# Cosine attention and a highway layer on one core: gate and highway products in PSUM, weights cast by DMA, last tiles in the score banks, late x turned by DMA, loads held back

## The chip, the cores and the metric

The kernel runs on one NeuronCore of a Trainium2 chip. The metric is the device time of one execution in microseconds. The profile's span, from the first to the last instruction, is about 2 us shorter than the device time.

## The reference

```python
# attention: q, k, v are (8, 12, 448, 64), float32; tau = 0.1
q_n = q / (norm(q) + 1e-6);  k_n = k / (norm(k) + 1e-6)
attn = softmax(q_n @ k_n.T / tau)              # over 448 keys
x = (attn @ v) as 3584 tokens x 768            # heads side by side
# highway layer: w_h, w_t are (768, 768), b_t is (768)
H = maximum(x @ w_h, 0)
T = 1 / (1 + exp(-(x @ w_t + b_t)))
out = T * H + (1 - T) * x                      # (3584, 768), float32
```

## The kernel before

The program names a *quad* Q: four heads of one batch element, 24 in all. A quad's q and k arrive by DMA as 32-bit tiles `raw`; sums of squares and an inverse root (Newton steps on VectorE) give `rs`; the product `qn` of `raw` and `rs` is made on GpSimd; `qT` is its transpose, by TensorE for the first four quads and by DMA for the others. Then come seven steps of scores (`sp`, two PSUM buffers of two banks each) with an exponential on ScalarE (`e`), the product with v (`u`, one buffer of two banks), and the division into `x`.

[...] 4 for `sp`, 2 for `u`, and 2 for `pt`, which the transposes of x (`xp`) and the highway products share.

```python
s_ps = pool("s_ps", 2, space=PS)
u_ps = pool("u_ps", 1, space=PS)
p_ps = pool("p_ps", 2, space=PS)
```

The 28 highway tiles of 128 tokens are numbered in order, three for each batch element and one of the leftover rows (`xtail`) for each pair of them. For each tile x is turned by TensorE, copied to SBUF, and multiplied by four half weights. The ones column of v holds 2.0, so that x is kept as x/2: the gate then is (1 + tanh(z))/2 with z from the product itself, and b_t enters halved as a seventh matmul with a row of ones.

```python
def tr():
    loc["xp"] = p_ps.tile([128, CC, 128], FP16, name="xp", tag="pt")
    for c in range(CC):                                                     # CC = 6
        nc.tensor.transpose(loc["xp"][:, c, :], xf()[:, c * 128 : (c + 1) * 128], ident[:, :])   # L729
def ev():
    loc["xT"] = xt_p.tile([128, CC, 128], FP16, name="xT")
    nc.vector.tensor_copy(loc["xT"][:, :, :], loc["xp"][:, :, :])           # L733
...
for qi, (w_i, mh) in enumerate(((1, 0), (0, 0), (1, 1), (0, 1))):           # w_i 1: gate, 0: highway
    ...
    nc.tensor.matmul(loc["pt", qi][:, :],                                   # L760, 128 x 384
        lhsT=loc["xT"][:, cc, :] if cc < CC else ones_row[:, :],
        rhs=w_f[w_i][:, cc, ms] if cc < CC else bth[:, ms], ...)
    ...
    nc.scalar.activation(loc["tt"][:, ms], loc["pt", qi][:, :], AF.Tanh)    # L780, w_i 1
    nc.vector.scalar_tensor_tensor(                                         # L785, w_i 0
        out=loc["hm"][:, ms], in0=loc["pt", qi][:, :], scalar=0.0,
        in1=xf()[:, ms], op0=ALU.max, op1=ALU.subtract)
...
nc.vector.scalar_tensor_tensor(                                             # L801
    out=loc["th", mh][:, :], in0=loc["tt"][:, ms], scalar=1.0,
    in1=loc["hm"][:, ms], op0=ALU.add, op1=ALU.mult)
nc.vector.scalar_tensor_tensor(                                             # L809
    out=loc["o"][:, ms], in0=xf()[:, ms], scalar=2.0, in1=loc["th", mh][:, :],
    op0=ALU.mult, op1=ALU.add)
```

So out = 2(x/2) + (1 + t)(max(h, 0) - x/2). Weights come as twelve loads into three staging buffers, and VectorE casts each to 16 bits:

```python
nc.sync.dma_start(st["wst", i][:, :], src[cc * 128 : (cc + 1) * 128, :])           # L302
nc.vector.tensor_copy(w_f[1 - i // CC][:, i % CC, :], st["wst", i][:, :])          # L305
```

The squares of k are made by GpSimd for quads under FOLD (VectorE for quad 0), and VectorE reduces all 64 of each group. From FOLD on, ScalarE squares both q and k, GpSimd adds halves twice (lines 397 and 403), and VectorE reduces 16:

```python
eng = "ACT" if t == 0 or Q >= FOLD else "POOL" if Q else "DVE"
```

All operations are put down with a duration, a due time and their dependences, and a list scheduler in Python fixes each engine's order while the program is built; on the chip that order is kept.

```python
k = (max(s, t + self.NEAR[e]), o.pri, o.n)       # s: earliest start, pri: due time
```

Of the kernel before, what the change touches and what calls it, by code (L numbers as in the profile page):

```python
# [20 lines left out]
class Plan:  # L21
# [7 lines left out]
    NEAR = {"PE": 100, "ACT": 100, "DVE": 60, "POOL": 60, "SP": 60}  # L29
# [23 lines left out]
    def run(self):  # L53
# [20 lines left out]
        while back:  # L74
            o = back.pop()
            due = 1e9 if o.pri is None else o.pri[0] if isinstance(o.pri, tuple) else o.pri
            for c in outs[o.n] if not isinstance(o.pri, tuple) else ():
                lat = o.dur + self.LAT[o.eng] + (o.size + 2000 if o.eng == "SP" else 0)
                due = min(due, c.pri - (self.SLACK * lat / 1000 if o in c.deps else 0))
            o.pri = due  # L80
            for d in o.deps + o.after:
                users[d.n] -= 1
                if not users[d.n]:
                    back.append(d)

        def arm(o):
            r = 0
            for d in o.deps:
                r = max(r, d.done + (100 if d.eng == o.eng else self.LAT[d.eng]))
            for d in o.after:  # L90
                r = max(r, d.start)
            if o.eng == "SP":
                r += 300
            ready[o.eng].append((r, o))
# [9 lines left out]
        while len(order) < len(self.ops):  # L104
            best = None
            for e, L in ready.items():
                if not L:
                    continue
                t = t_eng[e]
                pick = None  # L110
                for r, o in L:
                    s = max(t, r)
                    if e == "DVE" and o.kind == "lock":
                        s = max(s, port[0])
                    elif e == "POOL":
                        s = max(s, port[1])
                    elif e == "SP" and len(lanes) >= 8:
                        s = max(s, lanes[-8])
                    if e == "SP":
                        s = max(s, dma_free - 5000)  # L120
                    k = (max(s, t + self.NEAR[e]), o.pri, o.n)
                    if pick is None or k < pick[0]:
                        pick = (k, s, r, o)
                if best is None or pick[1] < best[1]:
                    best = pick
            _, s, r, o = best
            e = o.eng
            ready[e].remove((r, o))
            end = s + o.dur
            if e == "PE":  # L130
                if o.kind != mode:
                    end += self.SWITCH
                mode = o.kind
            elif e == "POOL":
                port[0] = end
            elif e == "DVE" and o.kind == "lock":
                port[1] = end
            t_eng[e] = end
            o.start, o.done = s, end
            if e == "SP":  # L140
                dma_free = max(dma_free, end + 900) + o.size
                o.done = dma_free + 1100
                lanes.append(o.done)
            order.append(o)
            for c in outs[o.n]:
                left[c.n] -= 1
                if not left[c.n]:
                    arm(c)
# [7 lines left out]
def kernel(  # L156
# [30 lines left out]
    wst_p = pool("wst", N_W)  # L187
# [23 lines left out]
    bt_raw = const.tile([1, DM], FP32)  # L211
    ones_row = const.tile([128, 128], FP16)
    NV = 2
    FOLD = 6
    PAIR = 0
    NEWT = 8
    LEVELS = 2
    PIECES = 2
    vm_b = [const.tile([128, 6, C, 66], FP16, name=f"vm{i}") for i in range(NV)]
# [36 lines left out]
    def load_qk(Q):  # L256
# [4 lines left out]
        for t in range(2):  # L261
# [10 lines left out]
            o = op("SP", 60 if Q == 0 and t else 550, None, wait, f, size=1300)  # L272
# [5 lines left out]
    def load_v(b):  # L278
        ring, wait = P.buf("vr", N_VR)
        st["ring_vr", b] = ring  # L280

        def f():
            st["vr", b] = vraw_p.tile([128, 6, C * D], FP32, name="vr")
            nc.sync.dma_start(
                st["vr", b][:, :, :],
                v[b].rearrange("n (p c) d -> (n p) (c d)", c=C).rearrange("(i x) f -> x i f", x=128),
            )

        o = op("SP", 600, None, wait, f, size=4000)
        ring.append(o)  # L290
        st["gotv", b] = o
# [3 lines left out]
    def load_w(i):  # L295
        ring, wait = P.buf("w", N_W)

        def f():
            st["wst", i] = wst_p.tile([128, DM], FP32, name="wst")
            cc = i % CC  # L300
            src = (moe_w_t, moe_w_h)[i // CC]
            nc.sync.dma_start(st["wst", i][:, :], src[cc * 128 : (cc + 1) * 128, :])  # L302

        def g():
            nc.vector.tensor_copy(w_f[1 - i // CC][:, i % CC, :], st["wst", i][:, :])  # L305

        a = op("SP", 430, (12 + 1.8 * i,), wait, f, size=1300)
        c = op("DVE", 470, (16 + 1.8 * i,), [a], g, kind="lock")
        ring += [a, c]
        w_done[1 - i // CC].append(c)  # L310

    def load_b():
        def f():
            nc.sync.dma_start(bt_raw[:1, :], moe_b_t)

        def g():
            nc.vector.tensor_single_scalar(bth[:1, :], bt_raw[:1, :], 0.5, ALU.mult)

        a = op("SP", 430, (20,), [], f, size=50)
        w_done[1].append(op("DVE", 470, (25,), [a, o_fb], g))  # L320
# [217 lines left out]
    def cast_v(b):  # L538
# [3 lines left out]
        for i in range(NQ):  # L542
# [5 lines left out]
            outs.append(op("DVE", 540, None, wait + [o_fv[b % NV], st["gotv", b]], f,  # L548
# [162 lines left out]
    def ffn(b, t, F):  # L711
# [11 lines left out]
        ringp, waitp = P.buf("pt", 2)  # L723
# [11 lines left out]
        a = op("PE", 300, None, need + waitp, tr, kind="full")  # L735
        c = op("DVE", 470, None, [a] + waitt, ev)
        ringp += [a, c]
        ringt.append(c)
        ring_x.append(a)
        return lambda later: quarters(b, t, F, loc, c, ringt, ring_x, xf, later)  # L740

    def quarters(b, t, F, loc, c, ringt, ring_x, xf, later):
        ringf, waitf = P.buf("ff", N_FF)
        ringo, waito = P.buf("o", N_O)
        last = {}
        for qi, (w_i, mh) in enumerate(((1, 0), (0, 0), (1, 1), (0, 1))):
            ms = slice(mh * MH, (mh + 1) * MH)
            if qi == 2:
                later()
            ringq, waitq = P.buf("pt", 2)  # L750
            prev = None
            when = F + 1.6 * qi
            groups = ((0, 1, 2), (3, 4, 5)) if w_i == 0 else ((0, 1, 2), (3, 4, 5, 6))
            mms = []
            for gi, grp in enumerate(groups):
                def mm(grp=grp, w_i=w_i, ms=ms, qi=qi):
                    if grp[0] == 0:
                        loc["pt", qi] = p_ps.tile([128, MH], FP32, name="pt", tag="pt")
                    for cc in grp:
                        nc.tensor.matmul(  # L760
                            loc["pt", qi][:, :],
                            lhsT=loc["xT"][:, cc, :] if cc < CC else ones_row[:, :],
                            rhs=w_f[w_i][:, cc, ms] if cc < CC else bth[:, ms],
                            start=(cc == 0), stop=(cc == CC - 1 + w_i),
                        )
                m = op("PE", 163 * len(grp), when + 0.5 * gi,
                       [c] + ([("first", mms[:1])] if mms else waitq) + w_done[w_i], mm, kind="full")
# [4 lines left out]
            def first():  # L772
                if "tt" not in loc:
                    loc["tt"] = ff_p.tile([128, DM], FP16, name="tt")
                    loc["hm"] = ff_p.tile([128, DM], FP16, name="hm")

            if w_i == 1:
                def fa(qi=qi, ms=ms):
                    first()
                    nc.scalar.activation(loc["tt"][:, ms], loc["pt", qi][:, :], AF.Tanh)  # L780
                e = op("ACT", 390, None, [mms[-1]] + waitf, fa)
            else:
                def fa(qi=qi, ms=ms):
                    first()
                    nc.vector.scalar_tensor_tensor(  # L785
                        out=loc["hm"][:, ms], in0=loc["pt", qi][:, :], scalar=0.0,
                        in1=xf()[:, ms], op0=ALU.max, op1=ALU.subtract,
                    )
                e = op("DVE", 470, None, [mms[-1]] + waitf, fa)
            ringq.append(e)  # L790
            ringf.append(e)
            ring_x.append(e)
            last[w_i, mh] = e
        fin = []
        for mh in range(2):
            ms = slice(mh * MH, (mh + 1) * MH)
            ringh, waith = P.buf("th", N_FF)

            def ft(ms=ms, mh=mh):
                loc["th", mh] = ff_p.tile([128, MH], FP16, name="th")  # L800
                nc.vector.scalar_tensor_tensor(  # L801
                    out=loc["th", mh][:, :], in0=loc["tt"][:, ms], scalar=1.0,
                    in1=loc["hm"][:, ms], op0=ALU.add, op1=ALU.mult,
                )

            def fo(ms=ms, mh=mh):
                if mh == 0:
                    loc["o"] = out_p.tile([128, DM], FP32, name="o")
                nc.vector.scalar_tensor_tensor(  # L809
                    out=loc["o"][:, ms], in0=xf()[:, ms], scalar=2.0, in1=loc["th", mh][:, :],  # L810
                    op0=ALU.mult, op1=ALU.add,
                )

            e1 = op("DVE", 470, F + 3.5 + 3.2 * mh, [last[0, mh], last[1, mh]] + waith, ft, kind="lock")
            e2 = op("DVE", 470, F + 4 + 3.2 * mh, [e1] + ([("first", fin[:1])] if fin else waito), fo, kind="lock")
            ringh += [e1, e2]
            ringf += [e1]
            ringo.append(e2)
            ring_x.append(e2)
# [14 lines left out]
    for Q in range(NQUAD):  # L834
# [3 lines left out]
        if Q == 1:  # L838
            for i in range(2 * CC):
# [23 lines left out]
    for b in range(B):  # L863
        f0 = slot_t[NQ * (b + 1)] + 5
        for t in [0, 1, 2] + ([3] if b % 2 else []):
            todo.append((b, t, f0 + 6.3 * t))
# [46 lines left out]
```

## Time and profile before

| | |
|---|---|
| device time, median of 3 runs | 314.18 us (312.53 to 314.8) |
| span of the profiled execution | 312.4 us |
| mean granted TensorE clock | 0.95 |
| DMA traffic | 58.59 MB, mean 188 GB/s |
| first and last exponential, start | 17.5 and 279.4 us |
| first and last highway matmul, start | 58.4 and 306.0 us |
| last product qn on GpSimd, start | 242.3 us |

The page gives busy times of the engines: PE is TensorE's matmuls, PEld its weight loads, DVE is VectorE, ACT ScalarE, POOL GpSimd, SP SyncE, which issues most DMAs. A busy PE is not PE at its peak, as matmuls are pipelined and their ends are modelled. The chain is the work that ended last, followed back from the last instruction to what released each step. A name such as L785 is a line of the kernel, and "out<-in" are its tiles.

### The profile page before, as it was taken

What the parts mean: (1) busy time and instruction counts of PE and PEld (TensorE: products, weight loads), DVE (VectorE), ACT (ScalarE), POOL (GpSimd) and SP (SyncE); (2) the same over time, 40 slices, a digit from 0 to 9 for tenths busy, and PEclk for the clock granted to TensorE, in tenths of its full rate; (3) what the DMA queues carried; (4) which work ended last, traced back from release to release, by engine and by line L of the source; (5) the groups of instructions that cost most, each with busy time, mean ns of one, the idle gap of its engine ahead of it and who ended that gap; (6) DMA issues with size and microseconds to landing.
All of it is one profiled execution on the core that took longest, in us unless ns stands there. A gap on an engine that the chain in (4) does not pass through costs nothing.

```text
span 312.4 us, 10165 instructions
## 1 busy us (share of the span) xinstructions
PE 252.9 (81%) x4312; PEld 144.3 (46%) x4312; DVE 256.6 (82%) x527; ACT 203.0 (65%) x267; POOL 179.8 (58%) x180
## 2 busy tenths in 40 slices
PE   0175485798786999889995999979888999998992
PEld 0133253354442555445543555545554555565551
DVE  2999997779976799899979777999998666666773
ACT  4175669378681897798789577977776767661110
POOL 0375789957993389957986869599559100000000
PEclk9999777599997899999999799999999999999997
DMA  7999945998998719992993299766624352201213
GB/s 268 406 344 327 370 126 159 368 294 270 229 242 275 266 25 241 245 352 43 237 263 148 40 290 282 253 111 111 111 68 86 125 65 69 78 23 37 101 51 101
DMA packets 62319, 58.59 MB, mean 188 GB/s; under 512 B 38721, under 2 KB 57153, under 8 KB 62274
## 3 DMA queue, kind: packets, MB, share of 16 engines
q1 hardware_dynamic: 62002, 57.49, 65.5%
q8 instruction: 33, 0.54, 0.7%
q10 hardware_dynamic: 272, 0.46, 0.4%
q14 instruction: 12, 0.10, 0.1%
HBM read 37.75 MB, written 11.01 MB: 156 GB/s over the span
## 4 chain that ended last, share of the span: by engine, by line
DVE 42%; PE 41%; POOL 9%; issue 4%; DMA 2%; ACT 1%; DVEq 0%; POOLq 0%; ACTq 0%
PE pt L760 26%; PE u L629 7%; DVE n L370 6%; PE sp L578 6%; POOL qn L489 5%; DVE th L801 5%; DVE vm L544 5%; DVE x L680 4%; DVE o L809 4%; DVE hm L785 4%; DVE ta L449 2%; POOL fold L397 2%; PE xp L729 2%; DVE ta L451 1%; DMA raw<-in_q_dram 1%
## 5 line engine op out<-in xcount | busy, mean ns | idle before, releaser
L589 ACT ACTIVATE e<-sp 128x896 f16<-128x896 f32 x168 | 144.9, 920 | 56.8 <-PE sp L578 56.7
L760 PE MATMUL pt<-w,xT 128*128 128x384 f16 x672 | 135.0, 335 | 9.7 <-DVE hm L785 7.8
L489 POOL TENSOR_TENSOR qn<-raw,rs 128x448 f16<-128x448 f32 x92 | 101.3, 1133 | 27.3 <-DVE rs L453 18.0
L760 PEld LDWEIGHTS <-xT 128*128 128x128 f16 x672 | 61.1, 99 | 62.5 <-issue 29.5
L629 PE MATMUL u<-vm,e 64*128 64x65 f16 x2688 | 57.8, 196 | 15.3 <-DVE x L680 14.0
L629 PEld LDWEIGHTS <-e 64*128 64x128 f16 x2688 | 49.1, 97 | 37.5 <-DVE x L680 18.3
L578 PE MATMUL sp<-qT,qT 64*64 64x448 f16 x672 | 54.1, 391 | 9.3 <-DVE qT L519 5.9
L397 POOL TENSOR_TENSOR fold<-sq 128x448 f32<-128x448 f16 x36 | 40.4, 1136 | 21.7 <-ACT sq L346 21.7
L780 ACT ACTIVATE tt<-pt 128x384 f16<-128x384 f32 x56 | 27.7, 494 | 34.6 <-PE pt L760 34.2
L785 DVE SCALAR_TENSOR_TENSOR hm<-pt,x 128x384 f16<-128x384 f32 x48 | 26.6, 554 | 25.5 <-PE pt L760 25.3
L346 ACT ACTIVATE sq<-raw 128x896 f16<-128x896 f32 x42 | 40.3, 963 | 10.3 <-DMA raw<-in_q_dram 9.1
L801 DVE SCALAR_TENSOR_TENSOR th<-tt,hm 128x384 f16<-128x384 f16 x56 | 42.1, 752 | 3.1 <-DVE ta L451 0.3
L809 DVE SCALAR_TENSOR_TENSOR o<-x,th 128x384 f32<-128x384 f16 x48 | 38.4, 799 | 0.8
L578 PEld LDWEIGHTS <-qT 64*64 64x64 f16 x672 | 14.2, 108 | 32.5 <-issue 23.4
L403 POOL TENSOR_TENSOR fold<-fold 128x224 f32<-128x224 f32 x36 | 27.9, 793 | 0.7
L680 DVE TENSOR_TENSOR x<-u,rd 128x384 f16<-128x384 f32 x48 | 24.8, 550 | 0.6
L544 DVE CAST vm<-vr 128x896 f16<-128x896 f32 x24 | 24.2, 1026 | 0.0
L370 DVE TENSOR_REDUCE n<-sq 128x7 f32<-128x448 f16 x24 | 13.9, 606 | 6.3 <-ACT sq L346 4.3
L760 PE MATMUL pt<-bth,ones_row 128*128 128x384 f16 x56 | 18.7, 333 | 0.0
L513 PE MATMUL tp<-ident,qn 128*128 128x128 f16 x56 | 6.2, 283 | 15.0 <-DVE qn L489 14.1
L729 PE MATMUL xp<-ident,x 128*128 128x128 f16 x144 | 13.1, 224 | 4.2 <-DVE x L680 4.2
L662 DVE RECIPROCAL rd<-u 128x12 f32<-128x12 f32 (+1 forms) x48 | 9.6, 201 | 7.6 <-PE u L629 6.9
(34 smaller groups left out, 133.6 us busy)
## 6 DMA issues: line engine op xcount, KB each, us to landing
raw<-in_q_dram SPq DMA_DIRECT2D x24, 448.0 KB, 4.9
vr<-in_v_dram SPq DMA_DIRECT2D x8, 1344.0 KB, 8.7
raw<-in_k_dram SPq DMA_DIRECT2D x23, 448.0 KB, 6.3
out_dram<-o SPq DMA_DIRECT2D x24, 384.0 KB, 3.1
wst<-in_moe_w_t_dram SPq DMA_DIRECT2D x6, 384.0 KB, 6.6
wst<-in_moe_w_h_dram SPq DMA_DIRECT2D x6, 384.0 KB, 5.4
out_dram<-o SPq DMA_DIRECT2D x8, 192.0 KB, 2.7
qT<-qn SPq DMA_TRANSPOSE x40, 4.6
```

Source lines behind the costliest of these rows:

```text
L346: nc.scalar.activation(o, i, AF.Square)
L397: nc.gpsimd.tensor_add(st["fold", Q, t][:, g, :], sq[:, g, 0 : D // 2], sq[:, g, D // 2 : D])
L489: (nc.vector if eng == "DVE" else nc.gpsimd).tensor_mul(st["qn", Q, t][:, :, :].rearrange("p c (h d) -> p h c d", h=2)[:, h0:h1, c0:c1, :] ...
L544: nc.vector.tensor_copy(vm[:, 2 * i : 2 * i + 2, :, 0:D], st["vr", b][:, 2 * i : 2 * i + 2, :].rearrange("p i (c d) -> p i c d", c=C),)
L578: nc.tensor.matmul(sp[64 * half : 64 * half + 64, h, 0:S].rearrange("x (c p) -> x c p", c=C), lhsT=kT[hp, ci, 64 * half : 64 * half + 64], ...
L589: nc.scalar.activation(e[:, o : o + 2 * S].rearrange("x (a p c) -> x a p c", a=2, c=C), st["sp", Q, ci][:, :, 0:S].rearrange("x a (c p) -> ...
L629: nc.tensor.matmul(u[:, s, slot * (D + 1) : (slot + 1) * (D + 1)], lhsT=e[sp, o : o + 128], rhs=vm[sp, 2 * qd + h, c, 0 : D + 1], start=(c ...
L680: nc.vector.tensor_mul(st["x", b][:, :, 4 * qd : 4 * qd + 4, :].rearrange("p t (h s) d -> p t h s d", s=2)[:, :, :, s, :], u[:, s, :, 0:D] ...
L760: nc.tensor.matmul(loc["pt", qi][:, :], lhsT=loc["xT"][:, cc, :] if cc < CC else ones_row[:, :], rhs=w_f[w_i][:, cc, ms] if cc < CC else b ...
L785: nc.vector.scalar_tensor_tensor(out=loc["hm"][:, ms], in0=loc["pt", qi][:, :], scalar=0.0, in1=xf()[:, ms], op0=ALU.max, op1=ALU.subtract,)
L801: nc.vector.scalar_tensor_tensor(out=loc["th", mh][:, :], in0=loc["tt"][:, ms], scalar=1.0, in1=loc["hm"][:, ms], op0=ALU.add, op1=ALU.mult,)
L809: nc.vector.scalar_tensor_tensor(out=loc["o"][:, ms], in0=xf()[:, ms], scalar=2.0, in1=loc["th", mh][:, :], op0=ALU.mult, op1=ALU.add,)
```

## The change

It has several parts.

1. *Gate and highway products.* out = max((1+t)h, 0) - (t-1)(x/2). VectorE makes the carry term g = (t-1)(x/2) in SBUF, multiplies h by (1+t) in place in PSUM, and then takes the maximum and subtracts g. It is meant to keep only one operation of a half tile with both inputs in SBUF.
2. *Weights.* Four DMAs issued by GpSimd cast while they load; the staging buffers and the casts on VectorE are gone.
3. *Last tiles.* Tiles 21 to 27 put gate and highway products side by side in one score buffer of two banks. Their bias is added by VectorE, from a copy of b_t on all partitions.
4. *Late x.* Tiles 17 to 23 are turned by a DMA transpose, without TensorE and the copy.
5. *Loads held back.* q, k and v are planned no sooner than 15 us before they are due, and v comes in thirds.
6. *Order and sizes.* The scheduler weighs due times more, FOLD goes from 6 to 9, the scores of the first six quads are issued singly (PAIR 6), and a tile's successor is turned ahead of the fourth quarter in place of the third (LATER 3).

The diff, with cuts:

```diff
-    NEAR = {"PE": 100, "ACT": 100, "DVE": 60, "POOL": 60, "SP": 60}
+    AHEAD = 15
+    NEAR = 60
+    LATE = 0.04
...
+            if o.kind == "load":
+                r = max(r, 1000 * (o.pri - self.AHEAD))
+            if o.kind == "at":
+                r = max(r, 1000 * o.pri)
...
-                    k = (max(s, t + self.NEAR[e]), o.pri, o.n)
+                    k = (max(s, t + self.NEAR) + (e != "SP") * self.LATE * 1000 * o.pri, o.pri, o.n)
...
-    bt_raw = const.tile([1, DM], FP32)
+    b_all = const.tile([128, DM], FP32)
-    FOLD = 6
-    PAIR = 0
+    FOLD = 9
+    PAIR = 6
+    LATER = 3
+    W_AT = 14
+    TAIL = 7
+    XDMA = (17, 24)
...
 (load_v: one DMA of 1344 KB becomes three of 448 KB, and each cast waits for its own)
...
 (load_w:)
-            nc.sync.dma_start(st["wst", i][:, :], src[cc * 128 : (cc + 1) * 128, :])
-            nc.vector.tensor_copy(w_f[1 - i // CC][:, i % CC, :], st["wst", i][:, :])
+            src = (moe_w_h, moe_w_t)[w_i].rearrange("(c p) f -> p c f", p=128)
+            cs = slice(3 * half, 3 * half + 3)
+            nc.gpsimd.dma_start(w_f[w_i][:, cs, :], src[:, cs, :])
...
+            nc.sync.dma_start(b_all[:, :], moe_b_t.partition_broadcast(128))
...
+        def td():
+            loc["xT"] = xt_p.tile([128, CC, 128], FP16, name="xT")
+            nc.sync.dma_start_transpose(loc["xT"][:, :, :], xf())
+        if XDMA[0] <= n < XDMA[1]:
+            c = a = op("SP", 1100, None, need + waitt, td, size=1140)
...
+            tail = n >= 28 - TAIL
+            if not tail:
+                ringq, waitq = P.buf("pt", 2)
+            elif w_i == 1:
+                ringq, waitq = P.buf("sp", 2)
-            groups = ((0, 1, 2), (3, 4, 5)) if w_i == 0 else ((0, 1, 2), (3, 4, 5, 6))
+            groups = ((0, 1, 2), (3, 4, 5)) if w_i == 0 or tail else ((0, 1, 2), (3, 4, 5, 6))
...
+                    def fb(qi=qi, ms=ms):                       # tail only
+                        nc.vector.scalar_tensor_tensor(
+                            out=loc["pt", qi], in0=b_all[:, ms], scalar=0.5, in1=loc["pt", qi],
+                            op0=ALU.mult, op1=ALU.add)
...
-                    nc.vector.scalar_tensor_tensor(
-                        out=loc["hm"][:, ms], in0=loc["pt", qi][:, :], scalar=0.0,
-                        in1=xf()[:, ms], op0=ALU.max, op1=ALU.subtract)
+                def fg(ms=ms, mh=mh):
+                    nc.vector.scalar_tensor_tensor(
+                        out=loc["g", mh][:, :], in0=loc["tt", mh][:, :], scalar=1.0,
+                        in1=xf()[:, ms], op0=ALU.subtract, op1=ALU.mult)
...
-                nc.vector.scalar_tensor_tensor(
-                    out=loc["th", mh][:, :], in0=loc["tt"][:, ms], scalar=1.0,
-                    in1=loc["hm"][:, ms], op0=ALU.add, op1=ALU.mult)
+            def fh(qi=qi, mh=mh):
+                h = loc["pt", qi]
+                nc.vector.scalar_tensor_tensor(
+                    out=h, in0=loc["tt", mh][:, :], scalar=1.0, in1=h, op0=ALU.add, op1=ALU.mult)
...
-                nc.vector.scalar_tensor_tensor(
-                    out=loc["o"][:, ms], in0=xf()[:, ms], scalar=2.0, in1=loc["th", mh][:, :],
-                    op0=ALU.mult, op1=ALU.add)
+                nc.vector.scalar_tensor_tensor(
+                    out=loc["o"][:, ms], in0=loc["pt", qi], scalar=0.0, in1=loc["g", mh][:, :],
+                    op0=ALU.max, op1=ALU.subtract)
...
-            e1 = op("DVE", 470, F + 3.5 + 3.2 * mh, [last[0, mh], last[1, mh]] + waith, ft, kind="lock")
+            e1 = op("DVE", 470, F + 3.5 + 3.2 * mh, [mms[-1], e], fh)
...
+            ringq += [e1, e2]
```

The last line says that a highway product's buffer is held until both of its operations are done.

## The prediction, made before the changed kernel was run

> **What bounds the kernel now.** I read the busy shares first, then one table of windows, then the chain, then single operations. Part 1 of the page gives, per engine, busy time, share of the span and instructions:
>
> ```profile
> PE 252.9 (81%) x4312; PEld 144.3 (46%) x4312; DVE 256.6 (82%) x527; ACT 203.0 (65%) x267; POOL 179.8 (58%) x180
> ```
>
> No engine is full, so the bound must change with the stage. The windows (start:end, length, busy us of each engine, granted clock, DMA share):
>
> ```profile
> 0.00:60.00 60.00, 29.25 (x513) 17.46 (x513) 50.92 (x125) 32.47 (x38) 37.89 (x42) 0.88 0.84 292
> 60.00:240.00 180.00, 159.57 (x2830) 89.22 (x2823) 158.68 (x309) 136.64 (x181) 138.37 (x136) 0.96 0.77 198
> 240.00:280.00 40.00, 40.00 (x722) 22.70 (x721) 26.80 (x56) 28.78 (x40) 3.54 (x4) 1.00 0.32 75
> 280.00:312.00 32.00, 24.05 (x259) 14.91 (x256) 20.21 (x40) 5.06 (x11) 0.00 (x0) 0.95 0.21 75
> ```
>
> The columns after the length are PE, PEld, DVE, ACT, POOL. **0 to 60 us** is a VectorE stage: 50.9 of 60 us, though it starts its real work only when q has landed at 5 us. **60 to 240 us** is a mixed one: PE and DVE are both at 88%, and they wait for each other. **240 to 280 us** is TensorE alone, 40.0 of 40. **280 to 312 us** is what the highway layer has left once the last exponential (start 279.4 us) is done. The chain says the same in shares of the span:
>
> ```profile
> DVE 42%; PE 41%; POOL 9%; issue 4%; DMA 2%; ACT 1%; DVEq 0%; POOLq 0%; ACTq 0%
> ```
>
> Then the highway layer's operations on VectorE. Each of the 56 half tiles has hm, th and o (lines 785, 801, 809), which have the same 384 elements a partition:
>
> ```profile
> L785 DVE SCALAR_TENSOR_TENSOR hm<-pt,x x48: 535/557/559, 64.0 to 302.1; 128x384 f16<-128x384 f32 x48
> L801 DVE SCALAR_TENSOR_TENSOR th<-tt,hm x56: 543/559/1422, 64.6 to 307.0; 128x384 f16<-128x384 f16 x56
> L809 DVE SCALAR_TENSOR_TENSOR o<-x,th x48: 516/559/1290, 68.4 to 303.4; 128x384 f32<-128x384 f16 x48
> ```
>
> The three numbers are ns, min/median/max. hm reads one tensor from PSUM and never takes more than 559. th and o read both tensors from SBUF; their floor is the same, but they reach 1422 and 1290. Windows by line show when: from 60 to 240 us, while GpSimd works, th took 30.43 us for 36 (845 ns) and o 32.26 for 36 (896), against 552 for hm; after 280 us, with GpSimd idle, 555 and 561.
>
> Last, the end. PE's own timeline shows tiles 5.03 us apart (the same step at 289.76, 294.79 and 299.82), with little free time:
>
> ```profile
> 294.18 0.56 DVE L785 SCALAR_TENSOR_TENSOR hm<-pt,x 128x384 f16<-128x384 f32 x1 [0.30 <-PE pt L760]
> 294.65 0.55 DVE L733 COPY xT<-xp 128x768 f16<-128x768 f16 x1
> 294.79 1.14 PE L760 MATMUL pt<-w,xT 128*128 128x384 f16 x6 [0.31 <-DVE hm L785]
> 295.12 0.55 DVE L801 SCALAR_TENSOR_TENSOR th<-tt,hm 128x384 f16<-128x384 f16 x1
> ```
>
> The first column is the start. 26 matmuls take 4.40 us in the chain (169 ns each), the six transposes about 0.5 us.
>
> [...]
>
> **The change part by part.**
>
> *Gate and products.* Per half tile, hm, th and o become g=(t-1)x, h=(1+t)h in place in PSUM, and o=max(h,0)-g. There are still three operations, but two of them now have a PSUM operand, so one instead of two can be blocked by GpSimd. In the middle stage 552+845+896=2293 ns become 845+555+555=1955, taking th's 845 for g and hm's 555 for the others: 338 ns a half, times 36 halves = **12.2 us of VectorE**. Late, with GpSimd idle, three times 555 remain three times 555. GpSimd, on the other side of the same lock, gets some time back, too (qn: 928 at best, 1225 median).
>
> *What that costs.* A highway product's PSUM buffer was free after one VectorE operation, and is now held until h and o are both done, one more of 0.56 us plus the queue before it. There are only two such buffers, and PE is in order. PE waited 7.8 us for hm in all; I allow +4 us over the 42 halves of the first 21 tiles, as score and value matmuls lie between.
>
> *Weights.* Twelve casts on VectorE go (9.0 us, mean 766 ns), 7.5 us of them before 60 us, where VectorE is the bound, and with them the three staging buffers behind which the Sync queue stood (9.0 us for line 302 on these casts). Four GpSimd DMAs come, of which I know no duration; GpSimd is idle 22 of the first 60 us. But the first highway matmul (58.4 us) waits for x, not for weights: so what counts is that attention's first three quads move up. I take 5 of the 7.5 us.
>
> *Squares.* FOLD 6 to 9 moves quads 6 to 8 back to plain squares: four reductions of 606 ns in place of two of 373 each, +1.7 us a quad, **+5.0 us** of VectorE; GpSimd drops two folds of 1136 and two of 793 for two squares of 1060, -1.7 us a quad, and ScalarE one square of 963 ns.
>
> *Late x by DMA.* Tiles 17 to 23 lose six transposes (0.5 us of PE) and the copy xT (0.55 of DVE): -3.5 us of PE, -3.8 of DVE. The transposes of qT took a median of 4.6 us to landing; they have a tile's time (5 us) to hide, and the DMA share there is 0.21 to 0.32.
>
> *Last seven tiles.* They take the score banks, which are free only after the last exponential; today about 4.75 tiles run after it. So 2.25 tiles x 4.9 = 11 us of PE work moves behind it, and what stood before it ends that much sooner. In itself this gains nothing. Each of these tiles loses two bias matmuls (2 x 0.165 us) but gets two additions of the bias on VectorE (2 x 0.56). VectorE then has 8 operations a tile, at 0.56 to 0.59 each **4.5 to 4.7 us**, plus 0.55 for the copy in the last four; PE has 24 x 0.169=4.06, plus 0.5. The end turns from PE-bound at 5.03 to VectorE-bound at about 4.9: -1 us over seven tiles.
>
> *Order.* Loads are held to 15 us before use, v comes in thirds, early scores come singly, and the list scheduler weighs due times. ScalarE waited 56.7 us for scores, so there is slack to win; I can't derive it and put it at -3 us.
>
> **The sum.** 0-60: -5. Middle: -12.2+5.0-1.5 (the last casts)=-8.7 of VectorE; at 88% busy this could be worth 10 us, but PE is equally full, so -8. From 240 us: -3.5 (transposes) and -1 give -4. Buffers +3 to +4, GpSimd's DMAs 0 to +1: call it +3. Order -3. Total -17: 314.2-17 = **297 us**. A check from the other side: VectorE's total becomes 256.6-9.0-12.2-3.8+5.0+7.8 = 244.4; at today's 82% that is 298 us.
>
> **Rivals.** (1) *PSUM becomes the wait*: if each of 42 halves stalls PE for 0.5 us, +21 us, and the time is back at 310 to 318. For it: VectorE is 88% busy, so h and o queue. Against it: PE has lost little on hm so far, 10 waits. (2) *VectorE relief is hidden*: the middle is PE-bound anyway, as 159.6 of 180 us suggests; then only the transposes, bias rows and a better start count, about -8, 306 us. Against it: PE's load is lower than its busy time, as a matmul's record is 326 ns long while they follow each other at 169, so every separate run of them counts up to 0.16 us too much. (3) *The lock was the trouble*: with half of the contended operations gone, GpSimd finishes its last qn (242.3 us) well earlier, scores come early and PE is filled all along; then 285 us. (4) *The end pays*: seven deferred tiles wait for the last exponential, and a slow one costs everything; +4 to +8.
>
> **Range and chances.** The parts move in one direction except for PSUM and the end; the order is the wide term. 297, 8 in 10 between 285 and 309. Faster by over 2% means below 307.9: 0.81; same 0.14; slower 0.05.
>
> **What would show it.** VectorE near 244 us, o with no time above some 570 ns, and only g spread up to 1400. No casts of w; first highway matmul near 53 us instead of 58.4. Last exponential near 255 us, and then seven tiles 4.5 to 5.2 us apart with DVE ahead of PE in the chain. PE's wait for o (instead of hm) below 15 us. The prediction is wrong if that wait is above 25 us, if h in PSUM takes well over 560 ns, if GpSimd's DMAs hold up qn by several us each, or if the last exponential is later than 265 us.

## The result, and the profile after

| | before | after |
|---|---|---|
| device time, median of 4 runs each | 313.36 us | 303.7 us (301.01 to 305.75) |
| ratio, with its 95% interval | | 0.966 (0.956 to 0.977) |
| span of the profiled execution | 312.4 us | 303.5 us |

Part 1 of the page of the changed kernel (busy time, share of the span and instructions of each engine), and the chain by engine:

```profile
PE 248.5 (82%) x4256; PEld 139.5 (46%) x4256; DVE 245.0 (81%) x528; ACT 201.5 (66%) x264; POOL 165.5 (55%) x178
...
PE 42%; DVE 33%; POOL 10%; issue 6%; ACT 5%; DMA 3%; SPq 0%; ACTq 0%; DVEq 0%; POOLq 0%
```

The table of windows of the same kernel (start:end, length, then busy us of PE, PEld, DVE, ACT, POOL; granted clock; DMA share and GB/s):

```profile
0.00:60.00 60.00, 30.17 (x514) 17.77 (x518) 51.82 (x115) 33.30 (x38) 33.67 (x43) 0.91 0.78 227
60.00:240.00 180.00, 169.34 (x3142) 93.84 (x3136) 149.93 (x326) 148.14 (x195) 131.84 (x136) 0.98 0.92 221
240.00:280.00 40.00, 35.41 (x529) 20.20 (x522) 27.27 (x58) 16.60 (x25) 0.00 (x0) 1.00 0.26 75
280.00:304.00 24.00, 13.60 (x88) 7.74 (x86) 15.99 (x32) 3.43 (x7) 0.00 (x0) 0.90 0.20 67
```

VectorE's total is 245.0, close to the 244.4 that was worked out. But the first window holds 51.8 us of VectorE work, 0.9 more than before, although the casts of the weights are gone. The middle window got fuller on PE (159.6 to 169.3) and on ScalarE (136.6 to 148.1). The operations that took the place of hm, th and o, on VectorE by line, with ns as min/median/max and the first and last start:

```profile
L815 DVE SCALAR_TENSOR_TENSOR g<-tt,x x48: 540/559/1291, 73.0 to 292.4; 128x384 f16<-128x384 f16 x48
L832 DVE SCALAR_TENSOR_TENSOR pt<-tt,pt x42: 541/555/564, 69.5 to 253.4; 128x384 f32<-128x384 f16 x42
L839 DVE SCALAR_TENSOR_TENSOR o<-pt,g x42: 543/556/559, 73.6 to 254.0; 128x384 f32<-128x384 f32 x42
```

As foreseen, only g, with two inputs from SBUF, is spread (up to 1291 ns); h in place in PSUM takes at most 564 ns and o at most 559, and GpSimd's product qn went from a median of 1225 ns to 936.

The useful table is one of stages, made from three events in each profiled execution: the start of the first highway matmul, the start of the last exponential, and the end of the span. Here with the experiments below except the fifth (times in us; device time is the median; the interval is that of the ratio to the kernel before as run beside it).

| kernel | first highway matmul | last exponential | from one to the other | after the last | device time | ratio (95% interval) |
|---|---|---|---|---|---|---|
| before | 58.4 | 279.4 | 221.0 | 33.0 | 313.4 | 1 |
| after | 61.5 | 255.1 | 193.6 | 48.4 | 303.7 | 0.966 (0.956 to 0.977) |
| after, h in SBUF | 61.5 | 257.4 | 195.9 | 47.3 | 306.75 | 0.981 (0.975 to 0.987) |
| after, old gate | 60.2 | 262.3 | 202.1 | 53.0 | 317.3 | 1.008 (1.005 to 1.012) |
| after, weights cast by VectorE | 73.1 | 260.0 | 186.9 | 48.6 | 309.6 | 0.986 (0.979 to 0.994) |
| after, FOLD 6 | 60.9 | 256.8 | 195.9 | 48.4 | 305.2 | 0.977 (0.970 to 0.984) |
| after, old order rules | 57.7 | 259.2 | 201.5 | 49.9 | 312.2 | 0.998 (0.994 to 1.002) |
| after, weight of due times 0.05 | 64.4 | 250.5 | 186.1 | 49.2 | 302.0 | 0.966 (0.960 to 0.971) |
| after, no tile in score banks | 55.6 | 263.6 | 208.0 | 31.3 | 296.4 | 0.947 (0.941 to 0.952) |
| the same, old gate | 55.8 | 264.8 | 209.0 | 30.7 | 299.75 | 0.957 (0.951 to 0.963) |
| after, due times not through banks | 55.9 | 255.7 | 199.8 | 52.6 | 310.4 | 0.992 (0.988 to 0.997) |
| before, new gate alone | 58.3 | 282.2 | 223.9 | 34.9 | 318.9 | 1.021 (1.014 to 1.028) |
| before, new order rules alone | 60.2 | 269.3 | 209.1 | 33.1 | 305.2 | 0.976 (0.970 to 0.982) |

The ratio leaves out executions over 1.5% slower than the fastest of the same kernel; with the old gate these were half of all, and the median of the others is 316.15 us.

From before to after the start lost 3.1 us, the stage between won 27.4, and the end lost 15.4. Some 2.25 tiles moved from the second to the third, so both of these numbers contain the move.

### The profile page after: what moved, and what is told of

It reads as the page before. It is cut to its first block, busy times and chain, and to the rows that moved or that the text cites. A ratio compares the mean times of both kernels' runs of the same rounds, so it can differ in the third digit from the quotient of the medians.

```text
span 303.5 us, 10013 instructions
## 1 busy us (share of the span) xinstructions
PE 248.5 (82%) x4256; PEld 139.5 (46%) x4256; DVE 245.0 (81%) x528; ACT 201.5 (66%) x264; POOL 165.5 (55%) x178
## 4 chain that ended last, share of the span: by engine, by line
PE 42%; DVE 33%; POOL 10%; issue 6%; ACT 5%; DMA 3%; SPq 0%; ACTq 0%; DVEq 0%; POOLq 0%
PE pt L782 17%; PE u L637 10%; PE sp L586 8%; DVE n L378 6%; PE sp L782 5%; POOL qn L497 5%; POOL fold L405 4%; DVE g L815 3%; DMA raw<-in_q_dram 3%; DVE x L688 3%; DVE vm L552 2%; DVE sp L801 2%; DVE o L839 2%; ACT e L597 2%; ACT tt L811 2%
## 5 line engine op out<-in xcount | busy, mean ns | idle before, releaser
L497 POOL TENSOR_TENSOR qn<-raw,rs 128x448 f16<-128x448 f32 x92 | 92.8, 1040 | 39.6 <-DVE rs L461 37.4
L782 PE MATMUL pt<-w,xT 128*128 128x384 f16 x504 | 98.9, 331 | 4.5 <-DVE xT L740 2.3
L637 PE MATMUL u<-vm,e 64*128 64x65 f16 x2688 | 58.3, 195 | 10.1 <-DVE xtail L680 3.6
L637 PEld LDWEIGHTS <-e 64*128 64x128 f16 x2688 | 49.2, 97 | 33.5 <-issue 19.6
L815 DVE SCALAR_TENSOR_TENSOR g<-tt,x 128x384 f16<-128x384 f16 x48 | 32.9, 686 | 13.1 <-ACT tt L811 12.8
L782 PE MATMUL sp<-w,xT 128*128 128x384 f16 x168 | 29.8, 326 | 7.3 <-DVE sp L801 3.6
L832 DVE SCALAR_TENSOR_TENSOR pt<-tt,pt 128x384 f32<-128x384 f16 x42 | 23.4, 556 | 9.1 <-PE pt L782 4.2
L811 ACT ACTIVATE tt<-sp 128x384 f16<-128x384 f32 x14 | 6.9, 490 | 34.8 <-DVE sp L801 19.3
L586 PEld LDWEIGHTS <-qT 64*64 64x64 f16 x672 | 14.5, 108 | 32.6 <-issue 24.1
L811 ACT ACTIVATE tt<-pt 128x384 f16<-128x384 f32 x42 | 20.8, 495 | 11.3 <-ACT e L597 5.4
L839 DVE SCALAR_TENSOR_TENSOR o<-pt,g 128x384 f32<-128x384 f32 x42 | 23.3, 556 | 1.3
L378 DVE TENSOR_REDUCE n<-sq 128x7 f32<-128x448 f16 x36 | 20.6, 606 | 4.1 <-ACT sq L354 4.0
L411 POOL TENSOR_TENSOR fold<-fold 128x224 f32<-128x224 f32 x30 | 21.1, 728 | 0.2
L521 PE MATMUL tp<-ident,qn 128*128 128x128 f16 x56 | 6.6, 290 | 15.7 <-DVE qn L497 13.6
```

The source lines that it names most:

```text
L378: nc.vector.reduce_sum(n2[:, qd, NT * t + g0 : NT * t + g0 + n], src()[:, g0 : g0 + n, 0:width], axis=AX.X,)
L497: (nc.vector if eng == "DVE" else nc.gpsimd).tensor_mul(st["qn", Q, t][:, :, :].rearrange("p c (h d) -> p h c d", h=2)[:, h0:h1, c0:c1, :] ...
L586: nc.tensor.matmul(sp[64 * half : 64 * half + 64, h, 0:S].rearrange("x (c p) -> x c p", c=C), lhsT=kT[hp, ci, 64 * half : 64 * half + 64], ...
L637: nc.tensor.matmul(u[:, s, slot * (D + 1) : (slot + 1) * (D + 1)], lhsT=e[sp, o : o + 128], rhs=vm[sp, 2 * qd + h, c, 0 : D + 1], start=(c ...
L782: nc.tensor.matmul(loc["pt", qi], lhsT=loc["xT"][:, cc, :] if cc < CC else ones_row[:, :], rhs=w_f[w_i][:, cc, ms] if cc < CC else bth[:, ms],
L811: nc.scalar.activation(loc["tt", mh][:, :], loc["pt", qi], AF.Tanh)
```

## The experiments

All are edits of the changed kernel unless said otherwise. Nearly every edit makes the list scheduler choose another order; where it doesn't, that is said. What runs is the order that was planned: in the changed kernel's trace VectorE's 528 instructions and PE's 4256 start in the order of the program.

**1. The lock alone, in the same order.** "The lock" is the prediction's name for a VectorE operation with two inputs from SBUF and one of GpSimd holding each other up. The two profiles show it in single times. In the kernel before, each of the 47 th and o that took over 600 ns ended 412 to 419 ns after an instruction of GpSimd had ended (one o began at 84.57 us and took 1.00, beside a fold on GpSimd from 84.50 that took 0.66), and each of the 48 qn over 1000 ns ended 786 to 800 ns after a th, an o, or a cast of v or of a weight had ended. In the changed kernel the same holds for the 21 g over 600 ns (413 to 418) and the 28 qn over 1000 (788 to 801, after a g or a cast of v), while 28 of the 56 h overlapped an instruction of GpSimd and none took over 564 ns.

In this experiment the operations and their planned order stay; only the place of h changes.

```diff
-                nc.vector.scalar_tensor_tensor(out=h, in0=loc["tt", mh], scalar=1.0, in1=h, ...)
+                loc["h", mh] = ff_p.tile([128, MH], FP32, name="hs")
+                nc.vector.scalar_tensor_tensor(out=loc["h", mh], in0=loc["tt", mh], scalar=1.0, in1=h, ...)
 ...
-                    out=loc["o"][:, ms], in0=loc["pt", qi], scalar=0.0, in1=loc["g", mh][:, :],
+                    out=loc["o"][:, ms], in0=loc["h", mh][:, :], scalar=0.0, in1=loc["g", mh][:, :],
```

> The changed kernel with the same order of instructions, but h=(1+t)h is written to SBUF in 32 bits instead of back to PSUM, so that o again has two SBUF inputs and the PSUM buffer is free one operation sooner. Theory 1, the lock between VectorE and GpSimd made the gain: o goes from 556 ns to 800 to 900 ns between 60 and 240 us and its maximum from 559 to over 1200, qn's median rises from 936 towards 1000 or more, and the time rises by 4 to 9 us, to 308 to 313. Rival, the longer hold of the PSUM buffers costs time: with the earlier release the time falls by 2 to 4 us, to about 300. Rival, the new order made the gain: no difference, within 1.5 us of 303.7.

The line of o in that kernel, by line as above:

```profile
L840 DVE SCALAR_TENSOR_TENSOR o<-hs,g x56: 550/559/1429, 71.8 to 300.0; 128x384 f32<-128x384 f32 x56
```

And part 1 of its page:

```profile
PE 245.8 (81%) x4256; PEld 138.8 (46%) x4256; DVE 261.3 (86%) x528; ACT 201.0 (66%) x264; POOL 174.6 (57%) x178
```

o is spread up to 1429 ns again (33.0 us for 37 between 60 and 240 us, 892 ns each, where the changed kernel has 556; 555 ns after 280 us, with GpSimd idle), VectorE works 16.3 us longer and GpSimd 9.1. The median of qn hardly moved (942 ns for 936, where 1000 or more was expected). The time rose by 3.0 us, below the range expected, and the stage between by 2.3; the intervals of the two kernels just overlap. So the lock is seen in VectorE's times, but only about a fifth of what it costs VectorE (3.0 of 16.3 us) shows at the end. An earlier release of the buffer came with the edit, so the lock's share may be a little larger.

**2. The old gate in the changed kernel.** hm, th and o again, in both kinds of bank.

```diff
-    g = (tt - 1) * x;  h = (tt + 1) * h (PSUM);  o = max(h, 0) - g
+    hm = max(h, 0) - x;  th = (tt + 1) * hm;  o = 2 * x + th
```

> The changed kernel with the old three operations (hm from PSUM; th and o with two SBUF inputs), all other parts kept. Theory 1 (the lock): two contended operations a half again, 12 us more VectorE time in the middle, time 309 to 313, most of the gain gone. Rival (order, tail, DMA parts made the gain): 303 to 306, with VectorE's busy time up and the time not.

12 to 14 us slower, more than expected, and the lock can't be all of it: the end, where GpSimd is idle, grew from 48.4 to 53.0 us. PE's waits for the bias show more of it, in that kernel and then in the changed one (us in total, times, longest):

```profile
PE sp L782 <- DVE sp L801: 10.2, 13, 0.8
```

```profile
PE sp L782 <- DVE sp L801: 3.6, 5, 0.9
```

In its order the highway product of a half comes behind the VectorE addition of that half's bias, and PE stands. So this run mixes the gate with the score banks, which is why experiment 10 repeats it without them.

**3. Weights cast by VectorE.** Twelve loads by the Sync queue into three staging buffers, and twelve casts.

```diff
-            nc.gpsimd.dma_start(w_f[w_i][:, cs, :], src[:, cs, :])
+            nc.sync.dma_start(st["wst", i][:, :], src[cc * 128 : (cc + 1) * 128, :])
+            nc.vector.tensor_copy(w_f[1 - i // CC][:, i % CC, :], st["wst", i][:, :])
```

> The changed kernel with twelve weight loads by the Sync queue and twelve casts on VectorE again. Theory: VectorE is the bound up to 60 us, so the 8 to 9 us of casts push the first highway matmul from 61.5 to 64 to 67 us and the time to 306 to 309. Rival: the casts fit beside waits, as the first highway matmul waits for x: time within 1.5 us of 303.7.

5.9 us slower, just above the theory's range, and the first highway matmul slid to 73.1 us, further than expected. In the changed kernel the four DMAs took GpSimd 0.77 to 0.93 us each and landed in 8.0 to 10.1 us.

**4. No tile in the score banks.**

```diff
-    TAIL = 7
+    TAIL = 0
```

> The changed kernel with no tile in the score banks: the last seven tiles take the two ordinary PSUM buffers and the bias as a seventh matmul. Theory: the end is bound by a chain through the bias on VectorE (tiles 5.35 us apart, Tanh waits 19 us for it), so without it the tiles are about 5.0 to 5.3 us apart and the time is equal or lower, 300 to 304. Rival: with only two buffers, each held until o is done, the steps grow to 6 us or more and the time to 307 to 312.

7.3 us faster, more than expected: the best kernel of this study. Part of it is the end, part the start, which the edit doesn't seem to touch. VectorE between 24 and 38 us shows the start. First the changed kernel, then this one (lines cut out of each timeline; first column the start, second the length):

```profile
28.05 1.66 DVE L378 TENSOR_REDUCE n<-sq 128x7 f32<-128x448 f16 x3
...
30.78 1.42 DVE L552 CAST vm<-vr 128x896 f16<-128x896 f32 x1
...
36.31 0.56 DVE L688 TENSOR_TENSOR x<-u,rd 128x384 f16<-128x384 f32 x1
```

```profile
24.38 0.62 DVE L552 CAST vm<-vr 128x896 f16<-128x896 f32 x1
...
28.48 1.02 DVE L688 TENSOR_TENSOR x<-u,rd 128x384 f16<-128x384 f32 x2
29.42 1.14 DVE L378 TENSOR_REDUCE n<-sq 128x7 f32<-128x448 f16 x2
```

With the score banks 16 reductions of squares stand ahead of the first cast of v, without them 12; the cast then comes 6.4 us sooner and the first x 7.8.

The last tiles are 5.28 us apart here (the same step, after the transposes, at 278.37 and 283.65 us) and 5.35 in the changed kernel (first gate matmuls at 286.93 and 292.28): nearly the same. But the end of the changed kernel has more tiles in it, and over all seven they are 6.15 us apart (first matmuls at 255.36 and 292.28), as products with v and the last divisions into x lie between. Its timeline over the last step:

```profile
289.10 0.56 DVE L801 SCALAR_TENSOR_TENSOR sp<-b_all,sp 128x384 f32<-128x384 f32 x1 [0.44 <-PE sp L782]
289.57 0.55 DVE L740 COPY xT<-xp 128x768 f16<-128x768 f16 x1
289.75 0.49 ACT L811 ACTIVATE tt<-sp 128x384 f16<-128x384 f32 x1 [2.75 <-DVE sp L801]
290.27 0.56 DVE L815 SCALAR_TENSOR_TENSOR g<-tt,x 128x384 f16<-128x384 f16 x1 [0.16 <-ACT tt L811]
290.75 0.55 DVE L832 SCALAR_TENSOR_TENSOR sp<-tt,sp 128x384 f32<-128x384 f16 x1
291.21 0.55 DVE L801 SCALAR_TENSOR_TENSOR sp<-b_all,sp 128x384 f32<-128x384 f32 x1
291.68 0.55 DVE L839 SCALAR_TENSOR_TENSOR o<-sp,g 128x384 f32<-128x384 f32 x1
292.28 0.99 PE L782 MATMUL sp<-w,xT 128*128 128x384 f16 x5 [1.28 <-DVE o L839]
```

Bias, Tanh, h and o follow one another, with g and the other half's bias between them on VectorE, and PE waits 1.28 us for o. The bank that was to free PE is held through a chain of four operations on two engines. That this chain, and not the number of tiles, made the loss isn't shown.

**5. The last tiles in the score banks, their bias by matmul.**

```diff
-            groups = ((0, 1, 2), (3, 4, 5)) if w_i == 0 or tail else ((0, 1, 2), (3, 4, 5, 6))
+            groups = ((0, 1, 2), (3, 4, 5)) if w_i == 0 else ((0, 1, 2), (3, 4, 5, 6))
```

> The changed kernel with the last seven tiles still in the score banks, but their bias as a seventh matmul in place of the addition on VectorE. Theory: the addition lies on the chain from the gate product to the Tanh and makes VectorE the bound of the end (8 or 9 operations a tile); without it a tile takes 4.9 to 5.1 us instead of 5.35, and the time falls by 2 to 3 us, to 301 to 302. Rival: PE is the bound of the end, and two more matmuls of 0.165 us a tile cost 2 us, 305 to 306.

304.4 us, ratio 0.974 (0.967 to 0.981). Neither came: the exchange of the addition on VectorE for two matmuls a tile made no difference that these runs can tell. Whether neither costs anything or both cost about the same isn't shown. The profiled execution of this kernel ran at a mean granted clock of 0.775, and its steps aren't read.

**6. The old rules of order.** The loads aren't held back either.

```diff
-    AHEAD = 15;  NEAR = 60;  LATE = 0.04
+    AHEAD = 10000;  NEAR = {"PE": 100, "ACT": 100, "DVE": 60, "POOL": 60, "SP": 60};  LATE = 0.0
```

> The changed kernel with the old rules of the list scheduler (near times of 100 for PE and ACT, no weight of due times, loads not held back), all operations as changed. My theory: the new order is a small part, and at the start it even costs; first highway matmul at 57 to 60 us, time 302 to 307. Rival (the order made the gain): 310 to 314.

312.2 us, the rival's range: with every operation as changed, 8.5 of the 9.7 us are gone. Which of the three settings did it wasn't tried.

**7. FOLD back at 6.**

```diff
-    FOLD = 9
+    FOLD = 6
```

> The changed kernel with FOLD back at 6. Theory: 12 reductions of 606 ns become 6 of 376, 5 us less on VectorE, of which 3 to 4 before 60 us where VectorE is the bound; first highway matmul at 58 to 60 instead of 61.5 us, time 301 to 304. Rival (GpSimd and ScalarE are what the start lacks): 305 to 308.

305.2 us, the intervals overlap: no difference that these runs can tell. VectorE had 3.0 us less (242.0), and it brought nothing.

**8. The new gate alone, in the kernel before.**

```diff
-    hm = max(h, 0) - x;  th = (tt + 1) * hm;  o = 2 * x + th
+    g = (tt - 1) * x;  h = (tt + 1) * h (PSUM, buffer held until o is done);  o = max(h, 0) - g
```

> The kernel before with only the first part of the change (g, h in place in PSUM, o from PSUM). Theory 1 (the lock): VectorE falls from 256.6 to about 246, g stays spread up to 1300 ns, o at 556; qn's median from 1225 to 950 to 1050; time 306 to 309. Rival (PSUM becomes the wait, with two buffers and transposes in between): PE waits for o 15 us or more, time 313 to 318. Rival (relief is hidden behind PE): 312 to 314.

2.1% **slower** (1.4 to 2.8), though VectorE fell from 256.6 to 244.7 us and GpSimd from 179.8 to 169.4; for VectorE, just as worked out. Of the 4.7 us that the span grew, 1.9 lie after the last exponential and 2.9 before it. PE's timeline near the end shows the first part:

```profile
298.77 1.14 PE L759 MATMUL pt<-w,xT 128*128 128x384 f16 x6 [0.78 <-DVE xT L733]
...
302.35 1.14 PE L759 MATMUL pt<-w,xT 128*128 128x384 f16 x6 [0.17 <-DVE o L804]
303.32 0.50 PE L729 MATMUL xp<-ident,xtail 128*128 128x128 f16 x6
304.60 1.14 PE L759 MATMUL pt<-w,xT 128*128 128x384 f16 x6 [0.78 <-DVE xT L733]
```

A tile takes 5.83 us here (298.77 to 304.60), against 5.03 before and 5.28 in the kernel of experiment 4. The step at 304.60 is a tile's third quarter, ahead of which its successor is turned (xp). It waits 0.78 us for the copy xT, where the same step before waited 0.31 for hm, and the second quarter waits 0.17 for o. PE's waits over the whole run, here and then before:

```profile
PE pt L759 <- DVE xT L733: 9.5, 8, 2.1
PE pt L759 <- DVE o L804: 8.0, 9, 2.0
```

```profile
PE pt L760 <- DVE hm L785: 7.8, 10, 3.1
PE pt L760 <- DVE xT L733: 1.9, 2, 1.3
```

Of these, 14.5 of 17.5 us lie ahead of 286 us here, and 8.7 of 9.7 before, so the loss isn't the end's alone. In experiment 4 the successor is turned a quarter of a tile later in the program (LATER 3), so that a gate product lies between h and the transposes, and PE's wait for o is 1.0 us in all. That this one setting makes the difference was not tried by itself. This kernel's order is another one, too, and part of its loss may be no more than that: experiment 11, with the operations of the changed kernel in another order, is 6.7 us slower than it, though at a lower clock, too.

**9. The new rules of order alone, in the kernel before.**

```diff
-    NEAR = {"PE": 100, "ACT": 100, "DVE": 60, "POOL": 60, "SP": 60}
+    AHEAD = 15;  NEAR = 60;  LATE = 0.04      # and q, k, v held until 15 us before they are due
```

> The kernel before with only the scheduler's new rules and the loads held to 15 us before they are due. Theory: order by itself is a large part; the new rules are worth what their removal cost the changed kernel, 6 to 8 us, 306 to 309. Rival, rules and sizes were fitted to the changed operations and do nothing for the old: 312 to 318.

305.2 us, 2.4% faster (1.8 to 3.0): with not one operation changed, most of the whole change's gain of 3.4%. Part 1 of its page and its chain:

```profile
PE 250.4 (83%) x4312; PEld 143.1 (47%) x4312; DVE 261.4 (86%) x527; ACT 203.6 (67%) x267; POOL 181.3 (60%) x180
...
DVE 58%; PE 34%; issue 3%; DMA 2%; ACT 1%; DVEq 0%
```

VectorE has even more to do than before (256.6), and is busy 86% instead of 82%: the gain is idle time that was filled. The stage between went from 221.0 to 209.1 us, with the same number of tiles left for the end (33.1 us against 33.0). GpSimd left the chain, where it had had 9%. The granted clock doesn't make the difference: executions at mean clocks of 0.949 to 0.955 took 304.3 to 305.8 us here, and those of the kernel before, run beside them, took 310.0 to 315.1 at 0.954 to 0.957.

**10. The old gate without the score banks.** Experiment 4 with the edit of experiment 2.

> The kernel without tiles in the score banks (296.4 us), with the old three operations of the gate again. Theory: VectorE carries 14 to 16 us more, of which the run with h in SBUF shows only 1 to 3 in the time; hm frees the PSUM buffer one operation sooner, which the end likes (tiles 5.0 instead of 5.28 us apart): 297 to 301. Rival, the gate was worth the 13 us that its removal cost beside the score banks: 306 to 311.

299.75 against 296.4 us, within the range expected. In a good order the gate is worth some 3 us, with intervals that just overlap (0.951 to 0.963, and 0.941 to 0.952), for 13.6 us of VectorE (251.4 against 237.8).

**11. Due times not carried through the score banks.** The last tiles still wait for the banks, but the list scheduler no longer makes the exponentials due early for their sake.

```diff
+                waitq = [("soft" if x[0] == "all" else x[0], x[1]) for x in waitq]   # waits, hands no due time back
```

> The changed kernel, its last seven tiles still in the score banks with the bias on VectorE, but the list scheduler no longer carries their due times back through the bank to the exponentials (they still wait for them). Theory: those due times pull scores, squares and reductions of later quads ahead of the casts of v, so that the first x comes at 36.3 instead of 28.5 us as without the score banks; then the first highway matmul comes at 55 to 57 us instead of 61.5 and the time is 297 to 300, the rest of the distance to 296.4 being the end itself. Rival, the score banks are slow in themselves: first highway matmul unchanged or time within 2 us of 303.7.

The first half held: the first highway matmul is at 55.9 us and the first x at 29.2, as without the banks. The due time that goes back through the bank is what spoilt the start. The second half fell: the time is 310.4 us. Without the pull, PE has no highway matmul from 243.7 us to the last exponential at 255.7, and the seven tiles find VectorE empty; its timeline there:

```profile
258.94 0.56 DVE L809 SCALAR_TENSOR_TENSOR sp<-b_all,sp 128x384 f32<-128x384 f32 x1 [5.47 <-PE sp L790]
261.24 0.56 DVE L823 SCALAR_TENSOR_TENSOR g<-tt,x 128x384 f16<-128x384 f16 x1 [1.73 <-ACT tt L819]
```

and PE's granted clock was 0.50 in all of the first 6.3 us of that stage:

```profile
255.70:262.00 6.30, 5.48 (x17) 2.46 (x17) 1.32 (x3) 1.39 (x3) 0.00 (x0) 0.50 0.00 0
```

Nine matmuls took 3.04 us there where the changed kernel has 1.64. At like clocks the two kernels are closer: three executions with a mean clock of 0.963 to 0.967 took 306.6 to 309.3 us, and the changed kernel took 305.8 and 305.3 at 0.960 and 0.965. So a part of the loss goes with the clock. How it divides, and why the clock fell, stays open.

**12. A small shift of the order.**

```diff
-    LATE = 0.04
+    LATE = 0.05
```

> A yardstick for the order alone: the changed kernel with the scheduler's weight of due times 0.05 instead of 0.04; no instruction is added, removed or altered, only some change places. Theory, the time depends on the order by several us: 304 to 311, away from 303.7 by more than 2. Rival, the order is a detail and the operations decide: 302.5 to 305.

302.0 us, ratio 0.966: no difference, though the first highway matmul came 2.9 us later and the stage between was 7.5 us shorter. So not every shuffle brings the 8.5 us of the rules. One shuffle doesn't measure what chance can bring, and in experiment 11 the same operations in another order, at a lower clock, took 6.7 us longer.

## Why the prediction was right, and where it wasn't

The time lay in the range and was called faster, but several terms were wrong and made up for each other: the gate and the start were taken for too much, the last tiles brought a loss, and the order brought the rest. That the sum still fell within 7 us of 297 is in part luck. By its steps:

- **"Gate and products": the relief was sized right, its worth was not.** VectorE came to 245.0 for 244.4 worked out; only g is spread. But a net relief of 8.7 us of VectorE in the middle (12.2 by the gate) was taken for 8 us of time. The same order with the lock back costs 3.0 us, the old gate in a good order 3.3, and the new gate alone loses 4.8 (318.92 against 314.14 in the same runs). The step that failed is "at 88% busy this could be worth 10 us, but PE is equally full, so -8": the two engines' busy shares of 88% don't say how much of one engine's work ends up in the time, and here it was 3.0 of 16.3 us (experiment 1) and 3.3 of 13.6 (experiment 10). Rival 2 (hidden relief) was nearer the truth.
- **"What that costs" (+3 to +4 us for the held buffers)** didn't show in the changed kernel: PE's waits for o sum to 5.7 us (pt 1.4, sp 2.5, xp 1.8), below the 15 us set as a test and below the 7.8 us for hm before. In the kernel before, the same operations cost 4.8 us in place of a gain, in the direction of rival 1, with 7.8 us more of PE's waits. That this turns on what stands next in the ring, the buffers of a pool taken in turn, fits the timelines of experiments 4 and 8 and isn't shown.
- **"Order", -3 us, "I can't derive it",** is the mis-sized term: the rules with the loads held back are worth 2.4% alone, some 7 to 9 us, and taking them away costs 8.5. PAIR, LATER and the thirds of v were not tried alone. The ScalarE waits of 56.7 us for scores, which were read as slack, didn't shrink with it (60.9 us in experiment 9), so that hint was no measure.
- **"0-60: -5" failed as a sum, and held as a part.** The weights are worth 5.9 us (experiment 3). But the first highway matmul came at 61.5 us instead of 53: the score banks' due times put 16 reductions of squares ahead of the first cast of v, where there are 12 without them. That 32 reductions and not 24 lie in the first 60 us is not the cause: the kernel of experiment 4 has 31 there and starts at 55.6 us, and that with FOLD 6 has 26 and starts at 60.9. The bias row alone took 2.94 us on VectorE for one partition, against 1.28 before; in the kernel of experiment 4 the same row took 0.54.
- **"Squares", +5 us of VectorE,** was no cost in time that could be told.
- **"Last seven tiles ... -1 us"** failed: the last tiles take 5.35 us, not 4.9, and all seven 6.15 on the mean; with the start they cost 7.3 us in all. The step that failed is the sum of busy times: the four operations of a half follow one another, and VectorE isn't full there (16.0 of the last 24 us), nor is PE (13.6). The last exponential was right to the microsecond (255.1 for "near 255"), but by luck: the start came 8.5 us later than foreseen and the middle made up for it.
- **Late x by DMA** was not tried alone; the DMA transposes landed in 2.9 us (x) and 4.5 (xtail), within the tile's time allowed for them.

## What to carry to other kernels

When two engines are each over 80% busy and neither is full, look at the order before the operations: here the same instructions in another order gave 2.4%, and 14 to 16 us less work on VectorE gave 1%. A buffer that is held one operation longer was free in one order and went with a loss of 4.8 us in another, so look at who uses it next. When a scarce buffer is lent to late work, ask two things: when is it free, and what does the wish to have it early do to everything ahead of it.

## What the runs showed of the hardware that was not expected

A VectorE operation that reads one of its operands from PSUM and writes its result back to the same place there (h) took a median of 555 ns for 384 elements of 32 bits in the changed kernel, and one that writes to SBUF (o) 556. A weight DMA of 576 KB that casts on the way took GpSimd 0.77 to 0.93 us to issue in the changed kernel, and landed after 8.0 to 10.1 us; in the kernel without score banks the issue took 0.80 to 1.15 us. The granted clock was 0.50 from 255.7 to 262 us in the kernel of experiment 11, across the change from scores to highway matmuls; in the changed kernel it was 1.00 from 252 to 262 us, across the same change. Why is open. That kernel's mean clock was 0.940 to 0.956 in 15 of its 18 executions, where the changed kernel has 0.960 to 0.986.
